# Attention and two mixture layers on one core: three rows of a step table are moved, the softmax sums are normalised at other steps, and a key difference on GpSimd is cut in two halves

## The chip, the cores and the metric

The kernel runs on one core of a Trainium2 chip, in one launch. The metric is device time in microseconds (us), from the start to the end of the execution; shorter is better. The engines are TensorE (PE in the profile, its weight loads PEld), VectorE (DVE), ScalarE (ACT), GpSimd (POOL) and SyncE (SP), which here only issues transfers: every DMA of the kernel goes through SP's queue, in program order.

## The reference

Three blocks, one after the other, in float32. The change is in the first.

```python
q_pool = q.reshape(B, H, S // 2, 2, D).mean(axis=3)          # B, H, S, D = 4, 8, 1152, 64
scores = 1/sqrt(D) * q_pool @ k.transpose(0, 1, 3, 2)
scores = scores - max(scores, axis=-1)
attn = exp(scores); attn = attn / (sum(attn, axis=-1) + 1e-09)
out = attn @ v                                               # 576 pooled queries, 1152 keys per head
...
x = out.transpose(0, 2, 1, 3).reshape(B, 576, 512)           # then two mixture layers of matmuls on x
```

## The kernel before

**Pairs and steps.** The 32 heads are worked in 16 pairs P = 0 to 15. A pair has 9 steps, one for each score tile of up to 128 queries by 1152 keys, so there are 144 steps; "step 3 of a pair" is step 9P + 3 (the diff calls them slots). One loop (line 568) writes each step out by hand, all engines in program order: in step s PE transposes the exponentials of tile s (L338), DVE and ACT copy the transposed thirds out of PSUM (L367), PE makes the scores of tile s + 2 (L304) into the PSUM banks that these copies have just freed, DVE takes their row maximum (L316, `smax`), ACT the exponentials (L328). In most steps PE also multiplies exponentials with values (L379, `pv`), 3 to 5 products of two heads each; some steps have none.

**Exact products in two parts.** Queries and keys are split in a high part, which the matmul takes as it is, and the rest. For a pair this is done one pair ahead, on POOL, in these steps: `qs` adds the two rows that are pooled (L232), `kh` cuts the keys (L197), `kl` is the difference keys minus cut keys (L200, tile kn, 128x1152), `qx` scales the queries (L239), `qh` cuts them (L197), `ql` is the difference of the queries (L200, tile qn). Then SP copies the parts to where the matmuls want them: `km`, four DMAs for the keys (L277, L278, tiles kt), and eight DMAs behind `ql` for the queries (L249 to L263, tiles q and qc). The keys and queries of the pair after that are loaded by `lqk` (L222, L223).

**Where a step's extra work stands.** The table `PREP` lists the steps at which these are issued: `(o, hook, name, ...)` means step o of the pair before; hook 0 is ahead of the step, hook 1 in its middle, hook 2 at its end. The first row of the table is for odd pairs (so it is worked during even ones), the second for even pairs. `CONV` is a like list for the conversion of the later layers' weights from float64, 20 pieces: a load by SP into tile cv (L122), an absolute value on ACT (L126), four bit operations on DVE (L129, L133, L137, L141), a rounding on ACT (L145), a difference on POOL (L149), and two stores by SP (L153, L154).

**Normalising.** When a pair's tiles are done, `norm1` takes the reciprocal of its 9 columns of sums on DVE: three small instructions (L393, L394, L395). SP then stores them in four DMAs to DRAM (L398) and reads them back spread over partitions in three (L407 to L409, tile rb). `norm2` multiplies the pair's output with that on POOL (L415). `NORM` says at which step `norm1` stands, counted from the pair's own first step, for even and odd pairs.

There is no scheduler: an engine does its instructions in the order in which this loop writes them, and waits only on semaphores.

Of the kernel before, what the change touches and what calls it, by code (L numbers as in the profile page):

```python
# [26 lines left out]
NP = NB * NH // 2  # L27
KT = S // 128
# [14 lines left out]
COPY = (('act', 'dve', 'act'), ('dve', 'act', 'act'), ('act', 'dve', 'dve'), ('dve', 'dve', 'act'))  # L43
SHORT = (0, 14, 16)
CLO = 'pool'
NORM = ((9, 2), (10, 2))

PREP = (
    ((-1, 2, 'qs', 'pool'), (1, 0, 'kh', 'pool', 0, 1), (1, 2, 'kl', 'pool', 0, 1), (2, 2, 'qx', 'pool'), (2, 2, 'qh', 'pool'), (2, 2, 'km', 0), (2, 2, 'km', 1), (3, 0, 'ql', 'pool'), (5, 0, 'lqk'), (15, 2, 'lv')),
    ((-1, 2, 'qs', 'pool'), (0, 2, 'kh', 'pool', 0, 1), (0, 2, 'kl', 'pool', 0, 1), (1, 2, 'qx', 'pool'), (2, 0, 'qh', 'pool'), (2, 0, 'km', 0), (2, 0, 'km', 1), (2, 2, 'ql', 'pool'), (5, 0, 'lqk'), (15, 2, 'lv')),  # L50
)

CONV = ((1, 2), (2, 1), (3, 2), (4, 1), (5, 2), (5, 2), (6, 1), (8, 1), (9, 2), (10, 1), (12, 1))
# [11 lines left out]
def attn_moe_kernel(ctx: ExitStack, tc: tile.TileContext, qT, kT, vP, muk, mur, wk, wv, wr, wth, wtr, wti, wch, ident, out):  # L65
    nc = tc.nc
    pe, act, dve, pool, sp = nc.tensor, nc.scalar, nc.vector, nc.gpsimd, nc.sync
# [90 lines left out]
    def attention(first):  # L158
# [258 lines left out]
        NT = NP * KT  # L417
# [3 lines left out]
        def at(slot, fn, *args):  # L421
            sched.setdefault(slot, []).append((fn, args))
# [13 lines left out]
        for P in range(NP):  # L436
            for g, (a, w, *when) in enumerate(groups):
                j = 0
                for o, m in when[P % 2]:
                    n = min(P * KT + o, NT)  # L440
                    plan.setdefault(n, []).extend(((P, g), j + x) for x in range(m))
                    j += m
                (at_mid if (n + 1) % 18 in SHORT else at_gap)(n + 1, pv_copy, (P, g))
            o, hook = NORM[P % 2]
            (at_gap, at_mid, at)[hook](min(P * KT + o, NT), norm1, P)
            at(n + (3 if P < NP - 1 else 6), norm2, P)
        last_slot = NT + 1

        def run_pv(s):
# [594 lines left out]
    with tc.manual_schedule():  # L1044
        dve.memset(hpi, math.pi / 2)
        act.activation(warm, hpi, AF.Exp)
        WR = [wr_tile(k).rearrange("p (a b) -> p a b", a=2) for k in range(4)]
        first = weight_pieces("wr", wr, 512, lambda name, k: WR[k], 512) + weight_pieces("wk", wk, 512, in_dram, 512)
        first += weight_pieces("wv", wv, 512, in_dram, 512)
        attention(first)  # L1050
# [37 lines left out]
```

## Time and profile before

| what | value |
|---|---|
| time before, median of 3 runs | 986.11 us (983.55 to 988.0) |
| the profiled execution's own time | 986.29 us |
| its span, first to last instruction | 984.2 us |
| PE busy | 958.6 us, 97% of the span |
| DVE, ACT, POOL busy | 694.9, 552.6, 450.7 us |
| the steps of attention | up to about 490 us of the span |

The profile is of one execution. A row that begins with an engine's name is a group or an instruction; `[1.15 <-DVE E L367]` behind a row of the timeline means that the engine stood idle for 1.15 us before it, and that the DVE instruction of line 367 which writes tile E ended the wait. `SPq` is an instruction of the queue of SP, that is, the issue of a DMA.

### The profile page before, as it was taken

To read this page: it belongs to the slowest core of one execution; us is meant where nothing else is said; L and a number is where in the kernel's file an instruction comes from. 1 tells how busy PE (TensorE), PEld (TensorE's weight loads), DVE (VectorE), ACT (ScalarE), POOL (GpSimd) and SP (SyncE) were. 2 spreads that over 40 slices of the span, in tenths; PEclk is the share of its full clock that TensorE was granted. 3 is DMA by queue.
4 is the path that set the end of the run, shared out by engine and by line. 5 is a ranking of instruction groups with operands and counts; after the bars stand their busy time and mean duration, and the time that the engine had idled before them with its cause. 6 is when DMAs were issued, how large, how long until landed. Compare 5 with 4: busy or idle time off the path is not lost.

```text
span 984.2 us, 18354 instructions
## 1 busy us (share of the span) xinstructions
PE 958.6 (97%) x6832; PEld 839.7 (85%) x6832; DVE 694.9 (71%) x1043; ACT 552.6 (56%) x1174; POOL 450.7 (46%) x454
## 2 busy tenths in 40 slices
PE   6999999999999999999999999999999999999998
PEld 4777777877777777777788999999999999999998
DVE  7577877787787788777747888878636755576622
ACT  5667666776666666667755566555535443343410
POOL 5314535234353234531226666555646666475731
PEclk8999999999999999999999999999999999999999
DMA  6666647866667775767373333323402501010001
GB/s 159 179 178 154 178 148 217 224 168 180 199 189 225 203 185 177 215 182 176 135 290 98 108 99 96 98 82 123 174 1 69 210 1 49 1 43 8 25 26 49
DMA packets 65641, 130.85 MB, mean 133 GB/s; under 512 B 14800, under 2 KB 33744, under 8 KB 65552
## 3 DMA queue, kind: packets, MB, share of 16 engines
q1 hardware_dynamic: 65552, 129.68, 45.4%
q8 instruction: 54, 0.88, 0.4%
q14 instruction: 35, 0.29, 0.1%
HBM read 70.98 MB, written 22.68 MB: 95 GB/s over the span
## 4 chain that ended last, share of the span: by engine, by line
PE 82%; DMA 6%; DVE 4%; SPq 4%; ACT 2%; POOL 1%; issue 1%; ACTq 0%; DVEq 0%; POOLq 0%
PE sc L304 13%; PE ps L981 12%; PE pv L379 11%; PE ps L731 10%; PE ps L750 10%; PE sc L338 8%; PE ps L1000 5%; PE ps L927 5%; PE ps L702 4%; PE tx L338 3%; DMA cv<-wv 2%; DVE m L316 1%; DMA q<-qn 1%; DMA cv<-wk 1%; DVE r L393 1%
## 5 line engine op out<-in xcount | busy, mean ns | idle before, releaser
L316 DVE TENSOR_REDUCE m<-sc 128x1 f32<-128x1152 f32 x144 | 195.4, 1357 | 71.7 <-PE sc L304 70.6
L328 ACT ACTIVATE e<-sc,m 128x1152 f32<-128x1152 f32 x144 | 176.0, 1222 | 76.4 <-DVE m L316 74.8
L304 PE MATMUL sc<-kt,q 128*128 128x384 f32 (+1 forms) x864 | 196.0, 354 | 14.6 <-DVE E L367 4.3
L304 PEld LDWEIGHTS sc<-kt,q 128*128 128x128 f32 (+1 forms) x864 | 143.5, 188 | 23.9 <-DVE E L367 6.2
L338 PEld LDWEIGHTS sc<-idn,e 128*128 128x128 f32 x864 | 98.3, 141 | 35.6 <-issue 27.7
L338 PE MATMUL sc<-idn,e 128*128 128x128 f32 x864 | 122.9, 279 | 2.3 <-ACT e L328 2.2
L981 PE MATMUL ps<-b,a 128*128 128x288 f32 x816 | 111.7, 296 | 0.0
L981 PEld LDWEIGHTS ps<-b,a 128*128 128x128 f32 x816 | 109.8, 188 | 0.6
L731 PE MATMUL ps<-x,a 128*128 128x288 f32 x768 | 105.7, 298 | 1.8 <-POOL x L682 1.5
L731 PEld LDWEIGHTS ps<-x,a 128*128 128x128 f32 x768 | 103.8, 191 | 2.6 <-POOL x L682 2.0
L750 PE MATMUL ps<-k,b 128*128 128x288 f32 x768 | 103.7, 295 | 0.0
L750 PEld LDWEIGHTS ps<-k,b 128*128 128x128 f32 x768 | 102.3, 188 | 0.3
L232 POOL TENSOR_TENSOR qn<-qn 128x576 f32<-128x576 f32 x15 | 22.1, 1476 | 145.4 <-DMA qn<-qT 85.5
L379 PE MATMUL pv<-M,vn 128*64 128x320 f32 x576 | 84.4, 438 | 0.0
L338 PE MATMUL tx<-idn,e 128*128 128x128 f32 x432 | 71.5, 275 | 0.5 <-DVE E L367 0.5
L379 PE MATMUL pv<-E,vn 128*64 128x256 f32 x576 | 71.0, 386 | 0.0
L379 PEld LDWEIGHTS pv<-M,vn 128*64 128x64 f32 x576 | 38.5, 136 | 36.1 <-issue 7.7
L718 POOL TENSOR_TENSOR k<-h,k 128x288 fp32r<-128x288 f32 x64 | 56.6, 900 | 19.5 <-ACT k L717 17.1
L367 ACT COPY M<-sc 128x384 f32<-128x384 f32 x104 | 46.0, 481 | 31.9 <-PE sc L338 31.9
L682 POOL TENSOR_TENSOR x<-t,x 128x288 fp32r<-128x288 f32 x56 | 47.9, 872 | 34.5 <-ACT x L681 32.6
L367 ACT COPY E<-sc 128x384 f32<-128x384 f32 x89 | 39.6, 481 | 42.0 <-PE sc L338 42.0
L149 POOL TENSOR_TENSOR cv<-cv 128x512 fp32r<-128x512 f32 x16 | 20.9, 1308 | 85.9 <-ACT cv L145 78.7
(128 smaller groups left out, 1649.4 us busy)
## 6 DMA issues: line engine op xcount, KB each, us to landing
vn<-vP SPq DMA_DIRECT2D x16, 576.0 KB
kt<-kh SPq DMA_DIRECT2D x31, 288.0 KB
kn<-kT SPq DMA_DIRECT2D x15, 576.0 KB
qn<-qT SPq DMA_DIRECT2D x15, 576.0 KB
kt<-kn SPq DMA_DIRECT2D x30, 288.0 KB
q<-qn SPq DMA_DIRECT2D x30, 288.0 KB
q<-qn SPq DMA_DIRECT2D x30, 256.0 KB
b<-wtk SPq DMA_DIRECT2D x9, 576.0 KB
```

Of the source, the lines that this page charges most:

```text
L304: r = pe.matmul(sc[0:m, c, 0:384], lhsT=x, rhs=k[:, 384 * c:384 * c + 384], start=(i == 0), stop=(i == len(ops) - 1),)
L316: r = dve.tensor_reduce(m, scs[n][:, :, 0:384], axis=AX.XY, op=ALU.max, negate=True)
L328: r = act.activation(e, sc[:, :, 0:384], AF.Exp, bias=m, scale=1.0, accum_out=rss[P][:, t:t + 1])
L338: r = pe.transpose(ps[:, 128 * j:128 * j + 128], es_[n][:, c, 128 * j:128 * j + 128], idn)
L367: r = (act.copy if e == "act" else dve.tensor_copy)(out, ps)
L379: pe.matmul(pvs[k][64 * h:64 * h + 64, :w], lhsT=vns[P][:, h, j], rhs=e, start=(x == 0), stop=(x == KT - 1))
L718: pool.tensor_tensor(q[:, 1], h, q[:, 0].bitcast(F32), ALU.subtract)
L731: pe.matmul(ps, lhsT=WK[k, f // 4][:, w, 128 * (f % 4):128 * (f % 4) + 128], rhs=x[k][:, c], start=(k == 0 and n == 0), stop=(k == 3 and n ...
L750: pe.matmul(pss[d], lhsT=WV[f][:, w, 128 * d:128 * d + 128], rhs=k2[f][:, c], start=(f == 0 and n == 0), stop=(f == 7 and n == 2))
L927: pe.matmul(ps, lhsT=y[k // 2][:, k % 2, x], rhs=WT[k][:, w], start=(k == 0 and p == 0), stop=(k == 3 and p == 2))
L981: pe.matmul(pss[d], lhsT=zs[j][z][:, 128 * d:128 * d + 128], rhs=WTK[min(j, 8)][:, w, cs], start=(m == 0 and n == 0), stop=(m == 8 and n = ...
L1000: pe.matmul(ps, lhsT=WC[k][:, w, 128 * d:128 * d + 128], rhs=us[c0, k][:, x], start=(k == 0 and n == 0), stop=(k == 3 and n == 2))
```

## The change

Numbers in three tables change, and how far ahead of `norm2` its `norm1` stands; no instruction's work does, but that `kl` is issued as two instructions of 576 columns.

```diff
-NORM = ((9, 2), (10, 2))
+NORM = ((13, 2), (16, 2))
...
-    ((-1, 2, 'qs', 'pool'), (1, 0, 'kh', 'pool', 0, 1), (1, 2, 'kl', 'pool', 0, 1), (2, 2, 'qx', 'pool'), (2, 2, 'qh', 'pool'), (2, 2, 'km', 0), (2, 2, 'km', 1), (3, 0, 'ql', 'pool'), (5, 0, 'lqk'), (15, 2, 'lv')),
...
+    ((-1, 2, 'qs', 'pool'), (1, 0, 'kh', 'pool', 0, 1), (1, 2, 'kl', 'pool', 0, 2), (1, 2, 'kl', 'pool', 1, 2), (2, 0, 'km', 0), (2, 0, 'km', 1), (2, 2, 'qx', 'pool'), (2, 2, 'qh', 'pool'), (2, 2, 'ql', 'pool'), (5, 0, 'lqk'), (15, 2, 'lv')),
...
-            at(n + (3 if P < NP - 1 else 6), norm2, P)
+            at(min(P * KT + o, NT) + (4 if P < NP - 1 else 6), norm2, P)
```

The second row of `PREP` changes in the same way. `norm1` of an even pair moves from step 0 to step 4 of the odd pair that follows, `norm1` of an odd pair from step 1 to step 7 of the even pair that follows; for the last pair nothing moves. `norm2` moves from step 5 of the pair that follows to its step 8 for an even pair, and from step 6 to step 2 of the pair after that for an odd one.

On DVE, the end of step 0 of pair 7, before (r is a tile of `norm1`, m the maxima, cv a weight piece, E the exponentials):

```order
L316 TENSOR_REDUCE m<-sc_121 128x1
L393 TENSOR_SCALAR r_140<-rs_137 128x9
L394 RECIPROCAL r_140<-r_140 128x9
L395 STREAM_TRANSPOSE rt<-r_140 128x32
L133 TENSOR_SCALAR cv<-cv 128x512
L367 COPY E<-sc_120 128x3x128
L137 SCALAR_TENSOR_TENSOR cv<-cv 128x512
```

The same place now:

```order
L316 TENSOR_REDUCE m<-sc_121 128x1
L133 TENSOR_SCALAR cv<-cv 128x512
L367 COPY E<-sc_120 128x3x128
L137 SCALAR_TENSOR_TENSOR cv<-cv 128x512
L316 TENSOR_REDUCE m<-sc_120 128x1
```

The end of step 4 now, from the copy ahead of it:

```order
L367 COPY M<-tx 128x3x2x64
L316 TENSOR_REDUCE m<-sc_121 128x1
L393 TENSOR_SCALAR r_140<-rs_137 128x9
L394 RECIPROCAL r_140<-r_140 128x9
L395 STREAM_TRANSPOSE rt<-r_140 128x32
L367 COPY M<-sc_120 128x3x128 x2
```

The bit operation L133 is now first behind the maximum, and `norm1` stands where two copies follow it and no bit operation.

On SP's queue, pair 14, before: the seven DMAs of `norm1` of pair 13 are ahead of the copies of keys and queries for pair 15.

```order
L398 DMA scr<-rt 9x32 x4
L407 DMA rb<-scr 64x576
L408 DMA rb<-scr 64x512
L409 DMA rb<-scr 64x64
L277 DMA kt<-kh 64x1152
L278 DMA kt<-kn 64x1152
L277 DMA kt<-kh 64x1152
L278 DMA kt<-kn 64x1152
L249 DMA q_1_0_125<-qn 64x1152
```

Now these copies come first; behind the last of them there follow a weight load, the values' load, two stores and only then `norm1`'s:

```order
L263 DMA qc_128<-qn 64x64 x2
L122 DMA cv<-wv 128x1024
L228 DMA vn<-vP 128x1152
L153 DMA wv_93<-cv 128x512
L154 DMA wv_93<-cv 128x512
L398 DMA scr<-rt 9x32 x4
L407 DMA rb<-scr 64x576
```

In an odd pair `norm1`'s seven DMAs moved likewise, and stand now between the last L263 and the loads L222 and L223.

On POOL the order of a pair's preparation stays. `ql` of odd pairs now comes ahead of the weight difference (L149) of its step, where there is one; for even pairs, `norm2` of an odd pair now stands between `qh` and `ql`.

## Rows read from the trace of the kernel before

**Rows 1.** The page's first part: busy time and share of the span.

```profile
span 984.2 us, 18354 instructions
PE 958.6 (97%) x6832; PEld 839.7 (85%) x6832; DVE 694.9 (71%) x1043; ACT 552.6 (56%) x1174; POOL 450.7 (46%) x454
```

**Rows 2.** Busy time by stretch; last columns granted clock, DMA share, GB/s.

```profile
34.00:490.00 456.00, 446.10 (x3215) 347.52 (x3213) 354.44 (x459) 311.84 (x575) 164.94 (x123) 1.00 0.67 184
```

**Rows 3.** Waits of PE from 34 to 490 us: total, times, longest.

```profile
PE sc L304 <- DVE E L367: 3.5, 3, 1.3
PE sc L304 <- DMA q<-qn: 3.0, 2, 1.8
PE sc L304 <- ACT M L367: 1.9, 1, 1.9
PE sc L304 <- ACT E L367: 1.1, 2, 0.7
```

**Rows 4.** Timeline of all engines, 226.2 to 231 us (pair 7, step 0).

```profile
226.27 2.64 POOL L200 TENSOR_TENSOR kn<-kn,kh 128x1152 f32<-128x1152 f32 x1
226.29 2.64 DVE L393 TENSOR_SCALAR r<-rs 128x9 f32<-128x9 f32 x1
229.22 0.21 DVE L395 STREAM_TRANSPOSE rt<-r 128x32 f32<-128x32 f32 x1
229.86 0.54 DVE L367 COPY E<-sc 128x384 f32<-128x384 f32 x1
230.45 0.64 PEld L304 LDWEIGHTS sc<-kt,q 128*128 128x128 f32 x4 [1.47 <-DVE E L367]
230.46 0.79 PE L304 MATMUL sc<-kt,q 128*128 128x384 f32 x3 [1.15 <-DVE E L367]
```

**Rows 5.** All instructions of line 393: shortest, median, longest in ns.

```profile
L393 DVE TENSOR_SCALAR r<-rs x16: 164/501/2644, 50.3 to 494.3; 128x9 f32<-128x9 f32 x16
```

**Rows 6.** Timeline of PE at 157 to 160 us: the first scores of pair 5.

```profile
159.21 0.97 PE L304 MATMUL sc<-kt,q 128*128 128x384 f32 x4 [1.26 <-DMA q<-qn]
```

**Rows 7.** Timelines of POOL, 438 to 445, and SP, 439 to 463 us (pair 14).

```profile
440.57 1.46 POOL L200 TENSOR_TENSOR qn<-qn 128x576 f32<-128x576 f32 x1
...
440.29 1.37 SPq L398 DMA_DIRECT2D scr<-rt  x4
448.16 1.33 SPq L249 DMA_DIRECT2D q<-qn  x1
456.01 0.59 SPq L122 DMA_DIRECT2D cv<-wv  x1
```

**Rows 8.** Timelines of ACT, 461 to 464, and PE, 461 to 465 us (pair 14, step 8).

```profile
461.70 0.66 ACT L126 ACTIVATE cv<-cv 128x512 f32<-128x512 f32 x1 [1.96 <-DMA cv<-wv]
...
463.98 0.62 PE L304 MATMUL sc<-kt,q 128*128 128x384 f32 x2 [1.86 <-ACT M L367]
```

**Rows 9.** Timelines of POOL, DVE, PE, 239 to 248 us (pair 7, steps 4 and 5).

```profile
241.92 1.28 POOL L149 TENSOR_TENSOR cv<-cv 128x512 fp32r<-128x512 f32 x1 [9.64 <-ACT cv L145]
...
240.61 1.36 DVE L316 TENSOR_REDUCE m<-sc 128x1 f32<-128x1152 f32 x1 [0.21 <-PE sc L304]
242.46 1.02 DVE L367 COPY M<-sc 128x384 f32<-128x384 f32 x2 [0.50 <-PE sc L338]
...
242.84 1.32 PE L304 MATMUL sc<-kt,q 128*128 128x384 f32 x6
```

**Rows 10.** Timelines of POOL, DVE, PE, 217 to 223 us (pair 6, steps 7 and 8).

```profile
219.96 1.28 POOL L149 TENSOR_TENSOR cv<-cv 128x512 fp32r<-128x512 f32 x1 [7.21 <-ACT cv L145]
...
218.76 1.36 DVE L316 TENSOR_REDUCE m<-sc 128x1 f32<-128x1152 f32 x1 [0.33 <-PE sc L304]
220.58 0.43 DVE L385 COPY xt<-pv 128x256 f32<-128x256 f32 x1 [0.46 <-PE pv L379]
221.05 0.56 DVE L367 COPY M<-sc 128x384 f32<-128x384 f32 x1
...
221.42 1.52 PE L304 MATMUL sc<-kt,q 128*128 128x384 f32 x6
```

More of the change, by code (lines that the diff above doesn't have):

```diff
@@ L45 @@
 CLO = 'pool'
-NORM = ((9, 2), (10, 2))
+NORM = ((13, 2), (16, 2))
 PREP = (
-    ((-1, 2, 'qs', 'pool'), (1, 0, 'kh', 'pool', 0, 1), (1, 2, 'kl', 'pool', 0, 1), (2, 2, 'qx', 'pool'), (2, 2, 'qh', 'pool'), (2, 2, 'km', 0), (2, 2, 'km', 1), (3, 0, 'ql', 'pool'), (5, 0, 'lqk'), (15, 2, 'lv')),
-    ((-1, 2, 'qs', 'pool'), (0, 2, 'kh', 'pool', 0, 1), (0, 2, 'kl', 'pool', 0, 1), (1, 2, 'qx', 'pool'), (2, 0, 'qh', 'pool'), (2, 0, 'km', 0), (2, 0, 'km', 1), (2, 2, 'ql', 'pool'), (5, 0, 'lqk'), (15, 2, 'lv')),
+    ((-1, 2, 'qs', 'pool'), (1, 0, 'kh', 'pool', 0, 1), (1, 2, 'kl', 'pool', 0, 2), (1, 2, 'kl', 'pool', 1, 2), (2, 0, 'km', 0), (2, 0, 'km', 1), (2, 2, 'qx', 'pool'), (2, 2, 'qh', 'pool'), (2, 2, 'ql', 'pool'), (5, 0, 'lqk'), (15, 2, 'lv')),
+    ((-1, 2, 'qs', 'pool'), (0, 2, 'kh', 'pool', 0, 1), (0, 2, 'kl', 'pool', 0, 2), (0, 2, 'kl', 'pool', 1, 2), (1, 2, 'km', 0), (1, 2, 'km', 1), (1, 2, 'qx', 'pool'), (2, 0, 'qh', 'pool'), (2, 2, 'ql', 'pool'), (5, 0, 'lqk'), (15, 2, 'lv')),
 )
```

## The prediction

> **What bounds the kernel now.** I began with the page's busy times: PE is busy for 958.6 of 984.2 us [rows 1], so only the 25.6 us in which it is idle can be won without taking work from it, and the change takes none. The change is all in attention, so I asked for the stretch from 34 us, behind the start, to 490 us, the end of the steps: 456.00 us, of which PE is busy 446.10, so idle 9.90 [rows 2]. That is the ceiling, 1.0% of the time. The waits of PE in this stretch tell what the 9.90 us are: 3.5 us in three waits for a copy by DVE, 3.0 in two for the copies of queries, 1.9 in one for a copy by ACT, 1.1 in two smaller ones for ACT [rows 3]; 0.4 us are spread over shorter gaps. PE's granted clock is 1.00 there [rows 2], its upper level, so the clock has no part in it. For each wait I went to the timeline, to see what the engine that PE waited for had done.
>
> **Waits for DVE (3.5 us).** At 226 us, step 0 of pair 7, DVE comes to `norm1`. Its first instruction, L393, works on 9 columns and took 2.64 us, from 226.29 to 228.93; on POOL `kl` (L200) runs from 226.27 to 228.91 [rows 4]. The shortest L393 took 0.164 us, the median 0.50 [rows 5]. So DVE stood for 2.5 us behind POOL's instruction, though no semaphore is between them. The copy of E, two instructions behind, came at 229.86, and PE, which needed that bank, stood for 1.15 us [rows 4]. The other two of the three waits are 60 and 120 us later, at the same step of pairs 9 and 11; that all three are 3.5 us is in [rows 3].
> The Trainium skill, SBUF — State Buffer, section Who interferes with whom, says that a DVE `tensor_scalar` with both ends in SBUF can use the port pair that it shares with GpSimd, and that the later of two then fully blocks until the first is done. By that rule L393 ends when L200 does, and the trace agrees to 0.02 us [rows 4]; the same rule speaks against the change too, since it blocks L393 behind any instruction of POOL, wherever it is moved.
> After the change, step 0 has no `norm1`. The bit operation that stands first in its place can be held by the same POOL work, but by no more than one half of `kl`, 2.64 / 2 = 1.3 us [rows 4], as POOL's instruction ends there. It is also spared `norm1`'s own time: from the end of L393 to the end of L395 there are 0.50 us [rows 4], with the shortest L393 0.66. So DVE comes out of the step at least 2.5 + 0.66 - 1.3 = 1.8 us earlier, more than the 1.15 us that PE lost. I take all 3.5 us as gone. (The weight loads stood a little longer, 1.47 us where PE shows 1.15 [rows 4], so the true loss may be 3.5 x 1.47 / 1.15 = 4.5 us.)
>
> **Waits for queries (3.0 us).** Pair 5's first scores waited 1.26 us for tile q [rows 6], pair 13's the rest of the 3.0 us [rows 3]. Pair 15's preparation, which goes the same way, shows why the copies are late: POOL is done with `ql` at 440.57 + 1.46 = 442.03, but SP issues `norm1`'s stores from 440.29, their read-backs and the keys' copies after that, and the first query copy at 448.16 [rows 7], 6.1 us after it could have gone. The change takes the seven DMAs out of the way, and puts the keys' copies ahead of `qx`, where they can go as soon as `kl` is done, while POOL works 2 us and more on the queries. So the query copies can start at `ql`'s end, some 6 us earlier in every odd pair. The waits are at most 1.8 us [rows 3]; they go. Even pairs, which show no such wait, gain the same. The loads of the pair after next are behind these copies, and in even pairs come earlier as well; in odd pairs `norm1`'s DMAs now stand ahead of them, which costs what they won. `norm2` between `qh` and `ql` waits for `norm1`'s read-back, which sets out four steps ahead of it; I cost it at nothing, since even pairs would have to lose their 6 us first.
>
> **Wait for ACT (1.9 us).** At 461.70 ACT's L126 had waited 1.96 us for a weight load, all that is behind it on ACT was late, and PE stood 1.86 us [rows 8]. That load was issued at 456.01, last in the queue behind pair 15's copies [rows 7]. With these some 6 us earlier, it lands before 461.70 - 1.96 = 459.7. Gone too. In all 3.5 + 3.0 + 1.9 = 8.4 us are taken away.
>
> **What the new places cost.** This is where I part from the plain sum. Steps 4 and 7 have no bit operation, but a short cover. In pair 7, step 4, the maximum ends at 241.97 and the next copies begin at 242.46; PE starts scores at 242.84, and needs the first copied bank two of six products later, 242.84 + 1.32 / 3 = 243.28. A free `norm1` of 0.66 us moves the first copy, half of 1.02 us, to 242.63 + 0.51 = 243.14: it just fits, so it costs nothing. But POOL's weight difference L149 stands there, from 241.92 to 243.20, and begins before L393 could [rows 9]. L393 would end at 243.20, `norm1` 0.50 later, the first copy at 244.21: PE waits 0.93 us. In pair 6, step 7, the maximum ends at 220.12 and L149 runs from 219.96 to 221.24; `norm1` would be done at 221.74, the copy L385 (0.43) and the copy of the bank (0.56) at 222.73, where PE needs it at 221.42 + 0.43 = 221.85 [rows 10]: 0.88 us. The conversion of weights has a period of eight pairs, so that pairs 14 and 15 repeat this, and the sum of the four is 2 x (0.93 + 0.88) = 3.6 us. At the eleven other places nothing of POOL's stood at that time in the trace of before. There POOL's preparation can come to stand, now that queries are loaded earlier in even pairs: between 0 and, at the four even pairs with a weight difference one step ahead, about half of such a wait, 4 x 0.45 = 1.8 us. I take 0 to 1.8 as the bound and 0.5 as the value, nearest to the many unharmed places. Cutting `kl` in two costs one more start on POOL per pair, for which the 64% of the stretch in which POOL is idle (164.94 of 456 busy [rows 2]) leave room: nothing. If that cover were gone, and a start cost as much as the shortest L393, 0.16 us [rows 5], 15 of them would be 2.4 us.
>
> **Sum.** 8.4 away, 3.6 + 0.5 new: 4.3 us won; with the higher reading of the waits for DVE 5.3. I take 5.0, for the high reading carries over to the other waits as well. The profiled execution took 986.29 us, so 981.3; it lies 0.2 us above the median 986.11, and so 981.1, in round numbers 981.
>
> **Rivals.**
> *The new places are free.* L149 and `norm1` could miss each other: at pair 7 they are 0.05 us apart (241.92 and 241.97 [rows 9]), and a DVE instruction that is first is not held. Then 8.4 to 9.9 us are won (all idle time of the stretch): 986.1 - 9 = 977. For it speaks the small distance at the odd pairs, against it that at pair 6 L149 is ahead by 0.16 us [rows 10].
> *New waits as dear as the old.* POOL's earlier work in even pairs meets `norm1` at step 7 in all seven of them and the four above keep theirs: 2 x 0.93 + 7 x 0.88 = 8.0 new against 8.4 gone. 985.5, no change that can be told.
> *Queries are late for another reason.* If it is the transfers and not their issue that are slow (the queues are busy 67% of the stretch [rows 2]), an earlier issue moves their landing less. Then the 3.0 us stay: 986.1 - 5.0 + 3.0 = 984.1. Against it: between 442.03 and 448.16 no query copy was under way at all [rows 7].
> *Slower.* In odd pairs SP now waits at `norm1`'s first store until DVE has done step 4, and the loads of keys and queries are queued behind it. If these loads then land late enough for the following preparation, done in even pairs, that the query copies lose more than the 6 us that they won, every odd pair's first scores wait longer. With copies 1.5 us later than before, that is 7 x 1.5 = 10.5 us more, less the 3.5 + 1.9 won elsewhere, and with the 4.1 at the new places: 986.1 + 9 = 995. It decides from the point at which SP is held at the store for over 6 us beyond the time at which it issued these loads before.
> The Trainium skill, DMA: Bandwidth & Descriptors, section Anatomy of one DMA, says that waits for semaphores are made by the issuing sequencer ahead of dispatch, so what is behind a waiting DMA in its queue waits too; by it the store does hold the loads. Rows 7 agree as far as they go: the eight DMAs behind the stores came after them, in order.
>
> **Chances.** My forecast 0.48, with its own range 978.5 to 983.5; the free places 0.20; new waits as dear 0.16; late queries 0.08; slower 0.08. A difference of 0.5%, 4.9 us, is about what a measurement of this kernel can tell from no change: faster is below 981.2, slower above 991.0. Half of the forecast's share and a little more lies below 981.2, with the free places some 0.47; slower 0.08; the rest, 0.45, within. For the range I go from the free places with all idle time won, 976, to the new waits as dear with a little on top, 986.5; less than 2 in 10 is left out, most of it the slower case.
>
> **What would show it.** In the changed kernel's trace: PE's waits from 34 to 490 us without a DVE wait at step 0 of pairs 7, 9 and 11, without a DMA wait on tile q at pairs 5 and 13, without ACT's wait at L126 in pair 14, step 8; the first query copy issued within 1 us of `ql`'s end in odd pairs; no L393 above 1.5 us, and L393 of about 1.2 us with a wait of PE behind it in pairs 6, 7, 14 and 15. I am wrong if PE's idle time in the stretch is under 3 or over 8 us, if a wait for q remains, or if PE's busy time itself changes.

## The result, and the profile after

The changed kernel takes 972.94 us, the median of four runs (971.16 to 977.12), against 985.64 us of four runs before: ratio 0.9874, 95% interval 0.9844 to 0.9903. So it is faster, by 12.7 us, where 5.0 were forecast. Its profiled execution took 971.99 us, 14.3 less than that of before. Ten single runs of the changed kernel, these four and six of the fifth experiment, lie between 971.2 and 978.8 us; the fifth experiment shows what differs between two of them. One more run of the kernel before, beside the first four experiments, took 1055.19 us at a mean granted clock of 0.848, and no comparison here uses it.

The page of the changed kernel begins with these lines (answering to [rows 1]):

```profile
span 969.9 us, 18358 instructions
PE 954.0 (98%) x6832; PEld 837.6 (86%) x6832; DVE 679.2 (70%) x1043; ACT 552.6 (57%) x1174; POOL 456.1 (47%) x469
```

The stretch from 34 to 490 us, as in [rows 2]; behind each engine's busy time stands its number of instructions:

```profile
34.00:490.00 456.00, 454.91 (x3294) 356.35 (x3293) 345.34 (x470) 318.40 (x594) 172.77 (x141) 1.00 0.69 193
```

PE is busy for 454.91 of the 456 us, and more of its instructions fit in, 3294 for 3215. Of the waits in [rows 3] only one of two for ACT is left (a wait of 0.3 us of a transpose, L338, is new):

```profile
PE sc L304 <- ACT E L367: 0.7, 1, 0.7
```

**Where the 14.3 us lie.** Row maxima (L316) mark the steps, one for each. The first row of each fence is, from the timeline of DVE, the maximum with which pair 1 begins; the second is the group of all 144, with the shortest, median and longest in ns and the start of the first and of the last. Before:

```profile
42.94 1.36 DVE L316 TENSOR_REDUCE m<-sc 128x1 f32<-128x1152 f32 x1 [0.21 <-PE sc L304]
...
L316 DVE TENSOR_REDUCE m<-sc x144: 1344/1358/1360, 8.7 to 487.5; 128x1 f32<-128x1152 f32 x144
```

After:

```profile
37.84 1.36 DVE L316 TENSOR_REDUCE m<-sc 128x1 f32<-128x1152 f32 x1 [0.21 <-PE sc L304]
...
L316 DVE TENSOR_REDUCE m<-sc x144: 1345/1358/1360, 8.9 to 471.1; 128x1 f32<-128x1152 f32 x144
```

The **start**, up to pair 1, went from 42.9 to 37.8 us; of the change only the preparation of pair 1 stands in it. The **steps** from there to the last maximum went from 444.6 to 433.3, that is 11.3 us less. The **tail** behind them went from 984.2 - 487.5 = 496.7 to 498.8, 2.1 more. 5.1 + 11.3 - 2.1 = 14.3.

**More than PE's idle time.** In the steps 11.3 us are won, where PE had 9.90 idle in the whole stretch [rows 2]. The row that explains it is that of the loads of weights (PEld) for the scores, from 43 to 488 us; behind the mean duration stands the idle time ahead of them. Before, and then after:

```profile
L304 PEld LDWEIGHTS sc<-kt,q 128*128 128x128 f32 (+1 forms) x804 | 131.9, 186 | 16.4 <-DVE E L367 4.8 <-DMA q<-qn 3.5 <-ACT M L367 2.5
```

```profile
L304 PEld LDWEIGHTS sc<-kt,q 128*128 128x128 f32 (+1 forms) x795 | 130.6, 186 | 5.0 <-DVE M L367 0.9 <-ACT M L367 0.3
```

The loads stood idle 11.4 us less. The three waits that I had priced at 3.5, 3.0 and 1.9 us of PE's idle time stand here with 4.8, 3.5 and 2.5. Counted gap by gap, those above 0.1 us between the two maxima, with those of the scores' other tiles (kh, qc), it is 13.6 before and 2.3 after, and the steps less this idle time are 431.0 us in both. For the ten profiles (the times come from three series of runs, the first two rows, experiments 1 to 4 and 5 to 8, and only within one were they taken side by side):

| kernel | time, median (runs) | start | steps | PE idle in the steps | L304 loads idle | steps less loads' idle |
|---|---|---|---|---|---|---|
| before | 985.64 (4) | 42.9 | 444.6 | 9.8 | 13.6 | 431.0 |
| after | 972.94 (4) | 37.8 | 433.3 | 0.7 | 2.3 | 431.0 |
| 1: both `norm1`, old `PREP` | 976.26 (4) | 43.3 | 436.5 | 2.5 | 5.9 | 430.6 |
| 2: new `PREP`, old `norm1` | 984.93 (10) | 43.6 | 441.2 | 7.2 | 10.3 | 430.9 |
| 3: `norm1` a little later | 981.61 (4) | 41.9 | 439.3 | 4.6 | 9.1 | 430.2 |
| 4: `kl` whole | 978.30 (4) | 42.7 | 434.5 | 1.6 | 3.7 | 430.8 |
| 5: as after | 977.72 (6) | 43.1 | 433.4 | 0.7 | 2.4 | 431.0 |
| 6: start's difference halved | 972.63 (6) | 38.6 | 433.9 | 1.2 | 3.0 | 430.9 |
| 7: even `norm1` alone | 988.17 (1) | 44.7 | 443.2 | 7.5 | 10.7 | 432.5 |
| 8: odd `norm1` alone | 976.22 (1) | 41.7 | 435.3 | 1.8 | 4.4 | 430.9 |

But for 7 (see there) the last column lies within 0.8 us, while the steps less PE's own idle time lie between 432.6 and 434.8. So the idle time of the loads is what the steps lose, and PE's own shows 72% of it before, 30% after, and from 29 to 70% elsewhere. Why PE's busy time covers the rest (the ends of its rows are modelled) was not tried. The Trainium skill, Perfetto Trace Analysis, section Identifying the Most-Contended Engine, says that the matmuls' busy share is not a good measure of how close a kernel is to its peak, since pipelined matmuls look smaller in the trace, and names the rate of matmul work and the busy share of the weight loads instead; the table agrees in that PE's busy time misleads, but what counts here is the idle time ahead of the loads.

**The new places.** Pair 7, step 4, where `norm1` now stands (to be held against [rows 9]):

```profile
232.12 1.36 DVE L316 TENSOR_REDUCE m<-sc 128x1 f32<-128x1152 f32 x1 [0.21 <-PE sc L304]
...
233.40 0.16 DVE L393 TENSOR_SCALAR r<-rs 128x9 f32<-128x9 f32 x1
233.44 1.28 POOL L149 TENSOR_TENSOR cv<-cv 128x512 fp32r<-128x512 f32 x1 [8.68 <-ACT cv L145]
```

Pair 6, step 7 (against [rows 10]):

```profile
211.80 1.36 DVE L316 TENSOR_REDUCE m<-sc 128x1 f32<-128x1152 f32 x1 [0.21 <-PE sc L304]
...
213.07 0.17 DVE L393 TENSOR_SCALAR r<-rs 128x9 f32<-128x9 f32 x1
213.11 1.27 POOL L149 TENSOR_TENSOR cv<-cv 128x512 fp32r<-128x512 f32 x1 [8.57 <-ACT cv L145]
```

The meeting that I foresaw takes place, but L393 comes 0.04 us ahead of L149, isn't held, and is over before it could matter. At pairs 14 and 15 it is the same (445.39 against 445.43, 466.63 against 466.67). It is no chance of one run: in the seven profiles in which L393 and L149 meet with nothing added (after, experiments 1 and 4 to 8) they meet 25 times, and each time L393 is 0.035 to 0.040 us ahead. All sixteen L393 (as [rows 5]):

```profile
L393 DVE TENSOR_SCALAR r<-rs x16: 161/164/589, 59.3 to 477.9; 128x9 f32<-128x9 f32 x16
```

**The queries' copies.** Timelines of POOL and SP, 425 to 436 us (pair 14, as [rows 7]):

```profile
429.28 1.42 POOL L200 TENSOR_TENSOR qn<-qn 128x576 f32<-128x576 f32 x1
...
428.54 0.77 SPq L278 DMA_DIRECT2D kt<-kn  x1
430.73 0.46 SPq L249 DMA_DIRECT2D q<-qn  x1
```

The keys' copies are issued when `ql` ends, at 429.28 + 1.42 = 430.70, and the first query copy goes 0.03 us later, where it had waited 6.1. Over the 14 later pairs it had gone 2.0 to 9.7 us after `ql`; now it goes 0.03 us after it in 12 of them, and 0.57 and 1.39 in two even ones.

### The profile page after: what moved, and what is told of

Same layout as the page of the kernel before. It is cut to its first block, busy times and chain, and to the rows that moved or that the text cites. A ratio compares the mean times of both kernels' runs of the same rounds, so it can differ in the third digit from the quotient of the medians.

```text
span 969.9 us, 18358 instructions
## 1 busy us (share of the span) xinstructions
PE 954.0 (98%) x6832; PEld 837.6 (86%) x6832; DVE 679.2 (70%) x1043; ACT 552.6 (57%) x1174; POOL 456.1 (47%) x469
## 4 chain that ended last, share of the span: by engine, by line
PE 94%; DVE 2%; DMA 1%; ACT 1%; issue 1%; SPq 0%; POOL 0%; ACTq 0%; POOLq 0%; DVEq 0%
PE sc L304 16%; PE pv L379 15%; PE ps L981 12%; PE ps L731 11%; PE ps L750 10%; PE sc L338 10%; PE ps L1000 5%; PE ps L927 5%; PE tx L338 5%; PE ps L702 4%; DVE m L316 1%; DMA a<-wth 1%; PE ps L885 1%; DMA kn<-kT 0%; ACT e L328 0%
## 5 line engine op out<-in xcount | busy, mean ns | idle before, releaser
L316 DVE TENSOR_REDUCE m<-sc 128x1 f32<-128x1152 f32 x144 | 195.4, 1357 | 67.4 <-PE sc L304 65.1
L304 PE MATMUL sc<-kt,q 128*128 128x384 f32 (+1 forms) x864 | 192.5, 351 | 4.2 <-DVE M L367 2.5
L304 PEld LDWEIGHTS sc<-kt,q 128*128 128x128 f32 (+1 forms) x864 | 142.0, 186 | 10.9 <-DVE M L367 3.7
L338 PEld LDWEIGHTS sc<-idn,e 128*128 128x128 f32 x864 | 97.2, 140 | 37.4 <-issue 28.5
L338 PE MATMUL sc<-idn,e 128*128 128x128 f32 x864 | 121.9, 277 | 3.7 <-ACT e L328 3.7
L338 PE MATMUL tx<-idn,e 128*128 128x128 f32 x432 | 70.7, 273 | 0.0
L379 PEld LDWEIGHTS pv<-M,vn 128*64 128x64 f32 x576 | 38.6, 136 | 36.1 <-issue 7.7
L415 POOL TENSOR_TENSOR xt<-xt,rb 128x576 f32<-128x576 f32 x16 | 22.9, 1432 | 98.8 <-DMA rb<-scr 56.7
L149 POOL TENSOR_TENSOR cv<-cv 128x512 fp32r<-128x512 f32 x16 | 21.2, 1327 | 96.3 <-ACT cv L145 96.3
```

The source lines that it names most:

```text
L304: r = pe.matmul(sc[0:m, c, 0:384], lhsT=x, rhs=k[:, 384 * c:384 * c + 384], start=(i == 0), stop=(i == len(ops) - 1),)
L316: r = dve.tensor_reduce(m, scs[n][:, :, 0:384], axis=AX.XY, op=ALU.max, negate=True)
L338: r = pe.transpose(ps[:, 128 * j:128 * j + 128], es_[n][:, c, 128 * j:128 * j + 128], idn)
L379: pe.matmul(pvs[k][64 * h:64 * h + 64, :w], lhsT=vns[P][:, h, j], rhs=e, start=(x == 0), stop=(x == KT - 1))
```

## The experiments

The first four ran side by side with 12 runs of the kernel before (983.7 to 988.8), the last four with 11 (median 986.73). Fences that give waits are of the stretch from 34 to 490 us. "Steps" and "start" are the table's.

**1. Both `norm1` moved, preparation as before.** The table `NORM` and the place of `norm2` as in the change, the table `PREP` as before.

```diff
-    (... (1, 2, 'kl', 'pool', 0, 2), (1, 2, 'kl', 'pool', 1, 2), (2, 0, 'km', 0), ...
+    (... (1, 2, 'kl', 'pool', 0, 1), (2, 2, 'qx', 'pool'), (2, 2, 'qh', 'pool'), (2, 2, 'km', 0), ...
```

> Only the normalising of sums is moved (steps 4 and 7); the preparation of keys and queries is as before, its key difference in one piece, its copies behind it. Theory A (the moved DMAs and the moved L393 make the whole gain): PE's waits for DVE at step 0 of pairs 7, 9 and 11, for q at pairs 5 and 13, and for ACT in pair 14 are all gone, PE idle from 34 to 490 us falls from 9.9 to under 2 us, time 9 to 12 us below before. Rival B (the preparation's new order and the halves are needed too): the bit operation that stands in norm1's place is held by the whole key difference, up to 2.6 us, and PE still waits some 1 us at step 0 of odd pairs; idle 3 to 5 us, time 5 to 8 us below before.

976.26 us, ratio 0.9899 (0.9865 to 0.9933); steps 436.5, 8.1 less than before. PE is idle for 2.9 us from 34 to 490 us, more than the 2 of theory A and just under the 3 of rival B. The one group over 0.3 us of its waits of PE that is new:

```profile
PE sc L304 <- DVE M L367: 1.7, 3, 0.7
```

The waits for queries and for ACT's weights, and those for DVE at step 0, are gone without the new `PREP`, and the query copies go at `ql`'s end as in the changed kernel; the three new waits for DVE are at step 7 of pairs 2, 8 and 10. At pair 8 the timeline of POOL and DVE has

```profile
276.36 2.64 POOL L200 TENSOR_TENSOR kn<-kn,kh 128x1152 f32<-128x1152 f32 x1
...
277.71 1.31 DVE L393 TENSOR_SCALAR r<-rs 128x9 f32<-128x9 f32 x1
```

`norm1` in its new place is held by the whole `kl` until that ends, at 279.00; at pairs 2 and 10 it is held likewise behind `kh` (L197) and `qs` (L232). So moving `norm1` is most of the gain, and the other part of the change removes some waits that this one brings.

**2. New preparation, `norm1` where it was.** The other half alone.

```diff
-NORM = ((13, 2), (16, 2))
+NORM = ((9, 2), (10, 2))
...
-            at(min(P * KT + o, NT) + (4 if P < NP - 1 else 6), norm2, P)
+            at(n + (3 if P < NP - 1 else 6), norm2, P)
```

> Only the preparation changes: key difference in two halves, key copies ahead of the queries' splitting; norm1 stays at steps 0 and 1, so its seven DMAs still stand ahead of the copies. Theory A: no L393 above 1.4 us, so the 3.5 us of waits for DVE go or fall below 1 us; the waits for q (3.0) and for ACT (1.9) stay, since the queue is as late as before. Time 3 to 4 us below before. Rival B (the early key copies are what makes the queries early): waits for q go as well, time 7 us or more below before.

984.93 us, ratio 0.998 (0.9966 to 0.9995); steps 441.2, 3.4 less than before. Waits of PE from 34 to 490 us, and the group of L393:

```profile
PE sc L304 <- DMA q<-qn: 4.1, 2, 2.7
PE sc L304 <- ACT M L367: 1.5, 1, 1.5
...
PE sc L304 <- DVE E L367: 0.4, 2, 0.2
...
L393 DVE TENSOR_SCALAR r<-rs x16: 161/486/1386, 51.0 to 491.6; 128x9 f32<-128x9 f32 x16
```

The waits for queries stay (4.1 for 3.0), and the first query copy of a pair still goes 0.8 to 9.5 us behind `ql` (pair 1's apart), so `km` ahead of `qx` doesn't free the queue: moving `norm1`'s DMAs does. The waits for DVE fall from 3.5 to 0.4, since L393 is held by one half of `kl` (1386 ns) and no longer by all of it (2644 [rows 5]). At pair 7, step 0, one comes during the first half:

```profile
226.60 1.41 POOL L200 TENSOR_TENSOR kn<-kn,kh 128x576 f32<-128x576 f32 x1
...
227.27 0.77 DVE L393 TENSOR_SCALAR r<-rs 128x9 f32<-128x9 f32 x1
...
227.97 1.41 POOL L200 TENSOR_TENSOR kn<-kn,kh 128x576 f32<-128x576 f32 x1
```

It ends at 228.04, with the first half (228.01), and doesn't wait for the second. Apart, the two parts take 8.1 and 3.4 us from the steps, together 11.3. That this nearly adds up is in part luck: each part alone removes the waits for DVE at step 0, and what is so counted twice is made up by the new waits of experiment 1, which the whole change doesn't have.

**3. `norm1` a little later.** Two one-column memsets on DVE ahead of L393, so that L149 is first where the two meet.

```diff
+            for _ in range(2):
+                dve.memset(r2[:, 31:32], 0.0)
```

> The changed kernel with two very short DVE instructions (a column of the sums' tile set to zero again) ahead of each norm1, so that L393 comes some 0.15 us later. Theory A (whoever comes first holds the other): in pairs 6, 7, 14 and 15 the weight difference on POOL is now first, L393 takes about 1.2 us there instead of 0.16, and PE waits 0.8 to 0.9 us behind each: 3.6 us in all, time 2 to 5 us above the changed kernel. Rival C (the new places have more cover than I reckoned): L393 is just as long, but PE waits under 0.2 us each, time within 1 us of the changed kernel. Rival D (no lock; L393 was long for another reason): L393 stays at 0.16 us.

981.61 us, ratio 0.9953 (0.9935 to 0.9971); steps 439.3, 6.1 more than after. Its lines stand 2 further down, so that L395 is `norm1`'s first instruction. Waits of PE, and the timeline at pair 7, step 4:

```profile
PE sc L304 <- DVE M L367: 3.6, 5, 0.8
...
238.67 1.28 POOL L149 TENSOR_TENSOR cv<-cv 128x512 fp32r<-128x512 f32 x1 [9.57 <-ACT cv L145]
...
238.78 1.19 DVE L395 TENSOR_SCALAR r<-rs 128x9 f32<-128x9 f32 x1
...
240.97 0.30 PEld L304 LDWEIGHTS sc<-kt,q 128*128 128x128 f32 x2 [1.10 <-DVE M L367]
240.97 1.08 PE L304 MATMUL sc<-kt,q 128*128 128x384 f32 x4 [0.78 <-DVE M L367]
```

The two memsets are 0.12 us of DVE's time at each `norm1` (59 ns each), and cost 6.1 us in all. L395 begins 0.11 us behind L149 and ends when that does, at 239.95 to 239.97, 1.03 us later than it would have; PE waits 0.78 us, the loads 1.10. This is the story that I had predicted for the change itself, with its price: 0.68 to 0.78 us of PE at each of the four places named, for the predicted 0.88 and 0.93. The fifth wait, 0.79 us at step 7 of pair 8, was not foreseen: there L395 begins at 278.39, behind the second half of `kl` (from 278.26), and takes 1.30 us; in the changed kernel it came ahead of that half and took 0.19. So the 3.6 us in all, as expected, are five smaller waits for four: in part luck. The Trainium skill, SBUF — State Buffer, section Who interferes with whom, has it that the engine which issues first keeps the shared pair for the whole instruction, and the other blocks; the trace agrees in both orders, with 0.16 us for L393 when it is 0.04 ahead, and 1.19 when it is 0.11 behind.

**4. `kl` in one piece.** All of the change but the halves.

```diff
-(1, 2, 'kl', 'pool', 0, 2), (1, 2, 'kl', 'pool', 1, 2)
+(1, 2, 'kl', 'pool', 0, 1)
```

> The changed kernel with the key difference in one piece again. Theory A: the bit operation at step 0 of odd pairs is held up to 2.6 us in place of 1.3, which the cover of 2.9 us of products there takes; PE idle from 34 to 490 us under 1 us, time within 2 us of the changed kernel. Rival B: PE waits 0.5 to 1 us at step 0 or 8 of most pairs, time 3 to 8 us above the changed kernel.

978.30 us, ratio 0.9918 (0.9901 to 0.9934); steps 434.5, 1.2 more than after, in one new wait of PE for DVE, 0.9 us, at pair 8, step 7. No wait at step 0 comes back, as theory A has it; PE is idle for 1.9 us from 34 to 490, not under 1. POOL and DVE there:

```profile
275.02 2.65 POOL L200 TENSOR_TENSOR kn<-kn,kh 128x1152 f32<-128x1152 f32 x1
...
276.17 1.52 DVE L393 TENSOR_SCALAR r<-rs 128x9 f32<-128x9 f32 x1
```

Halving is worth 1.2 us here once `norm1` stands at its new places (0.6 against the 433.9 of experiment 6, whose steps are the changed kernel's). The other 4.9 us by which this profile differs (a start of 42.7 for 37.8) could be the whole `kl` of pair 1, which is worked in the start, or not the kernel's at all; that led to the next two.

**5. The changed kernel again.** Two import lines are exchanged, no instruction differs:

```diff
+import math
 from contextlib import ExitStack
 
-import math
```
The question was whether the start of 37.8 us belongs to the change.

> The changed kernel once more, as it is (two import lines exchanged). Theory F (the changed kernel's profiled start, 5 us shorter than before's, is a matter of which of POOL and DVE comes first, and not of the change): the start, to the first row maximum of pair 1, falls on either 37 to 38 us or 42 to 44 us in this profile, and the single times lie in two groups some 5 us apart, about 972 and 977. Rival G (the change shortens the start): 37 to 38 us here too, and all times near 972. From pair 1's first row maximum to the last one: 433 us, as in its first profile, by either.

977.72 us (975.30 to 978.79, six runs), ratio 0.9918 (0.9891 to 0.9946). The steps repeat to 0.1 us (433.4), the start doesn't: 43.1, as before. Rival G is refuted. Two groups of times, as theory F has it, don't stand out: the ten runs of this kernel go from 971.2 to 978.8 with no gap over 2 us. What differs, in the timelines of POOL, DVE and PE at 9 to 17 us, is a race of the same kind. In this run:

```profile
9.71 1.40 POOL L492 TENSOR_TENSOR qn<-qn 64x576 f32<-64x576 f32 x1 [0.24 <-DMA qn<-qT]
11.07 2.87 POOL L200 TENSOR_TENSOR kt<-kn,kh 64x1152 fp32r<-64x1152 f32 x1
...
10.27 4.02 DVE L500 SCALAR_TENSOR_TENSOR q<-qn,q 64x320 fp32r<-64x320 f32 x2
...
14.34 0.62 PE L304 MATMUL sc<-kt,q 128*128 128x384 f32 x2 [1.32 <-DVE q L500]
```

and in the changed kernel's first profile:

```profile
9.09 1.16 POOL L197 TENSOR_SCALAR kh<-kn 64x1152 fp32r<-64x1152 f32 x1 [6.09 <-DMA kn<-kT]
10.22 1.74 POOL L492 TENSOR_TENSOR qn<-qn 64x576 f32<-64x576 f32 x1
11.92 2.90 POOL L200 TENSOR_TENSOR kt<-kn,kh 64x1152 fp32r<-64x1152 f32 x1
...
10.22 2.08 DVE L500 SCALAR_TENSOR_TENSOR q<-qn,q 64x320 fp32r<-64x320 f32 x2
...
10.71 1.60 DVE L500 SCALAR_TENSOR_TENSOR q<-qn,q 64x320 fp32r<-64x320 f32 x1
...
12.72 0.60 PE L304 MATMUL sc<-kt,q 128*128 128x384 f32 x2
```

The row with x2 holds two L500; the 10.71 row is the second of them by itself. In this run POOL's L492 is ahead of the first, which ends at 11.46, and its difference of the first keys (L200) begins at 11.07, ahead of the second (11.47), which is held until that ends; the pair takes 4.02 us. In the first profile the keys' load landed later (POOL waited 6.09 us for it; 5.32 in this run), and L492 began together with the first L500, which took 0.47. The second, from 10.71, took 1.60: it ends 0.34 us behind L492 (11.96), so it was held by that alone, and L200 came behind it, at 11.92. So something is held in both profiles, and the pair takes 2.08 or 4.02 us; in all ten the second L500 ends 0.34 to 0.36 us behind the POOL instruction that began ahead of it. PE then waits 1.32 us or not at all. The windows from 15 to 20 us have, in this run and then in the first profile of the changed kernel,

```profile
15.00:20.00 5.00, 3.81 (x16) 3.71 (x17) 3.80 (x5) 3.49 (x7) 1.73 (x2) 0.66 0.46 182
```

```profile
15.00:20.00 5.00, 3.90 (x28) 3.17 (x26) 4.66 (x6) 2.91 (x8) 1.09 (x4) 1.00 0.56 220
```

a granted clock of 0.66, so partly at the lower level of 1.2 GHz, against 1.00; 16 matmuls stand in the one and 28 in the other. In the profile of before POOL's difference also began at 11.07 and the two L500 took 4.28. In all ten profiles the two go together: where the two L500 took 3.6 to 4.3 us (eight profiles) the start is 41.7 to 44.7, where they took 2.08 and 2.48 it is 37.8 and 38.6. So one kernel has both starts, and the 5.1 us are no part of what the change does in the steps, though they are in the 14.3 between the two profiles. Whether the change makes the short start more frequent, no run tells; of the kernel before, one run of the eleven beside this experiment took 978.97 us, 4.2 less than the next.

**6. The start's difference halved too.** As L200 at the start was suspected, it is cut in two halves in the changed kernel, like `kl`.

```diff
-            cut_lo("pool", kt1[h1], k[h1], kh[h1])
+            for c in (left, right):
+                cut_lo("pool", kt1[h1, c], k[h1, c], kh[h1, c])
```

> The changed kernel, and at the start the key difference of the second head (line 200, tile kt, 2.9 us on POOL) in two halves. Theory F: the second query rest on DVE (line 500) waits for one half of it at most, PE's first scores of tile 2 begin some 1.4 us earlier where POOL comes first, the granted clock does not fall at 13 us, and the start is 38 to 40 us in every run: times near 972 and less spread, 3 to 5 us below the changed kernel where that had the long start. Rival H (the start is bound by the loads and by the other waits, 1.8 us for the first exponentials and 2.3 us at step 1): time within 1 us of the changed kernel.

972.63 us, ratio to the kernel before 0.9876 (0.9845 to 0.9907), 5.1 us below the changed kernel's six runs beside it; five of its six runs are at 974 or less, of the ten runs of the changed kernel three. Start 38.6.

```profile
12.29 1.67 POOL L200 TENSOR_TENSOR kt<-kn,kh 64x576 fp32r<-64x576 f32 x1
...
10.19 2.48 DVE L500 SCALAR_TENSOR_TENSOR q<-qn,q 64x320 fp32r<-64x320 f32 x2
```

The two L500 take 2.48 us, and PE doesn't wait for them. In this profile POOL came late as well (12.29), so the trace doesn't show a half holding the second L500, and the order of the first profile, with the whole L200, would have done the same. PE's granted clock fell all the same, for 3.4 us from 11.9, where theory F had it not fall. That halves bound the loss in the other five runs is not shown; the times, 0.5% below those of the changed kernel beside it, speak for it.

**7 and 8. Each `norm1` alone.** In the kernel before, with its `PREP`: only that of even pairs moved, and only that of odd pairs, each with its `norm2`.

```diff
-NORM = ((9, 2), (10, 2))
+NORM = ((13, 2), (10, 2))
```

> The kernel before, with norm1 and norm2 of even pairs alone moved (to steps 4 and 8 of the odd pair). Theory A: the DVE waits at step 0 of pairs 7, 9 and 11 go (3.5 us shown), the waits for q at pairs 5 and 13 (3.0) and for ACT in pair 14 (1.9) stay, since in even pairs the seven DMAs are still ahead of the copies; PE idle from 34 to 490 us 5 to 7 us. Rival B: the loads in odd pairs, now behind the DMAs, make the waits for q longer than 4 us.

988.17 us, one run, within the runs of the kernel before beside it (978.97 to 988.58); steps 443.2, only 1.4 less than before.

```profile
PE sc L304 <- DMA q<-qn: 4.2, 2, 2.6
PE sc L304 <- DVE E L367: 2.2, 3, 1.8
PE sc L304 <- ACT M L367: 1.1, 1, 1.1
...
440.39 2.63 POOL L200 TENSOR_TENSOR kn<-kn,kh 128x1152 f32<-128x1152 f32 x1
...
440.75 2.55 DVE L133 TENSOR_SCALAR cv<-cv 128x512 uint32<-128x512 uint32 x1
```

The waits at step 0 of pairs 7, 9 and 11 are gone, but at pair 14 a bit operation takes 2.55 us beside the whole `kl`, and PE waits 1.80 for the copy behind it. The waits for queries stay, and their 4.2 us meet rival B's mark of 4. The wait for ACT is no longer in pair 14 but in pair 6, and PE is idle for 8.2 us from 34 to 490, above the 5 to 7 expected. Behind the wait of 1.80 PE's granted clock is 0.50, its lower level, for 3.4 us from 445.3; no other profile has that in its steps. With it go the 1.5 us by which this row of the table stands above the others, so the gain in the steps would be nearer 3 us by an estimate from the table (1.4 + 1.5).

```diff
-NORM = ((9, 2), (10, 2))
+NORM = ((9, 2), (16, 2))
```

> The kernel before, with norm1 and norm2 of odd pairs alone moved (to step 7, and step 2 of the pair after). Theory A: the waits for q and for ACT in pair 14 go, the DVE waits at step 0 of odd pairs stay at 3 to 4 us shown; PE idle from 34 to 490 us 4 to 6 us.

976.22 us, one run; steps 435.3, 9.3 less than before.

```profile
PE sc L304 <- DMA q<-qn: 0.4, 1, 0.4
...
PE sc L304 <- DVE E L367: 0.2, 1, 0.2
```

The queries' and ACT's waits go, as expected, but for 0.4 us at one place; PE is idle for 2.2 us, where 4 to 6 were expected. That the waits for DVE at step 0 of odd pairs would stay was wrong: `norm1` still stands there, but isn't held for long. The timelines of pair 7 show why:

```profile
221.87 2.65 POOL L200 TENSOR_TENSOR kn<-kn,kh 128x1152 f32<-128x1152 f32 x1
...
223.92 0.63 DVE L393 TENSOR_SCALAR r<-rs 128x9 f32<-128x9 f32 x1
```

`kl` is 4.4 us earlier than in [rows 4] and L393 only 2.4: with the queue free in even pairs, the loads issued there (L222, at 209.09 for 216.70 before) seem to land earlier, and POOL begins its preparation sooner: ahead of `qs` (L232) it stands idle for 2.40 us before, and not at all here. So the odd `norm1` makes most of the gain, and the even one, moved on top of it, costs 1.2 us as long as `kl` is whole (steps 435.3 here, 436.5 in experiment 1, whose three waits stand at step 7; one profile of each). How it brings these about was not followed.

## Why the prediction was right or wrong

**What was right.** The direction and the mechanisms. L393's 2.64 us were a stand behind POOL and no work (experiments 1 to 3), though no semaphore is between the two; that an engine waits only on semaphores, as is said of the kernel before, does not hold for DVE beside POOL. The waits for queries came from `norm1`'s DMAs ahead of the copies in SP's queue (experiments 1 and 8 against 2 and 7), and the copies now go at `ql`'s end. ACT's wait at L126 fell with them. The loads that stand behind `norm1`'s store, the rival *Slower*, made PE wait nowhere, nor did any other wait at the queue. Each of the rows named as signs was found, but for the last, an L393 of 1.2 us in pairs 6, 7, 14 and 15.

**The step that failed: what the new places cost.** 3.6 + 0.5 = 4.1 us were charged, 0 were paid in the two profiles of the changed kernel; the rival "the new places are free" had this right. I put the earliest begin of `norm1` in pair 7 at 241.97, the end of the maximum's row, and L149 0.05 us ahead of it. But on DVE the next instruction begins 0.08 us before that row's end: after the change L393 begins at 233.40, where the maximum's row ends at 232.12 + 1.36 = 233.48. The trace of before has the same, 0.076 to 0.086 us, all 101 times that an instruction follows a maximum at once. By that, DVE was free at 241.89, 0.03 ahead of L149. In pair 6 the same 0.08 would not have been enough against 0.16; there L149 came 1.31 us behind the maximum's begin where it had been 1.20 ([rows 10] and the fence above), which fits that the maximum waited 0.21 us for PE in place of 0.33. Experiment 3 shows that all else in this step held: let L149 be first, and the four waits stand where they were foreseen and cost about what was said. So the order was wrong and not the price, and it was no toss: the 25 meetings went the same way. The 0.5 for the other places was not idle either: in experiment 6, whose steps are the changed kernel's, L393 at step 7 of pair 12 comes 0.24 us behind `qs` (L232), takes 1.20 us, and PE waits 0.47. With the trace of before alone, an order within 0.05 us should have been given as open, with 981 and 977 as its ends, and not as one case. Two figures of the working are also off by little: in pair 6 a third of the 1.52 us shown is 0.51 and not 0.43, which makes that wait 0.80, and the rival *New waits as dear as the old* comes to 985.7 and not 985.5.

**A term mis-sized: the waits removed.** I priced them with PE's idle time, 8.4 us, where the loads show 4.8 + 3.5 + 2.5 = 10.8, and called the 9.90 of [rows 2] a ceiling. The loads of weights lost 13.6, and the steps gained 11.3, so that the range, whose lower end of 976 stood on that ceiling, was too high. The remark in the step on DVE, that 1.47 stands where PE shows 1.15, was the right reading, for all waits and not for one. It follows that "wrong if PE's busy time itself changes" was a bad test, since part of the wait is counted there as busy.

**What lay outside it.** With both corrected, 986.3 - 11.3 is 975.0. The rest, 5.1 us of start less 2.1 of tail, is not what was predicted, and the start differs between two profiles of one kernel (experiment 5). Beside the runs of experiment 5 the change is worth 9.0 us (0.9918). The tail took 497 to 499 us in all ten profiles; in the changed kernel's first profile PE's granted clock was at its lower level for 6.8 us from 504.9, before for 3.4 us at 521.5. That is not all of it, as the six other tails with 3.4 us go from 497.1 to 498.7; what makes them differ was not tried, and it stays open.

## What to carry to other kernels

Read a wait of PE from the idle time of its weight loads, and check it against the length of the stage: here that came out at 11.3 us, where PE's own idle time said 9. An instruction of a few columns on DVE costs what is left of the POOL instruction beside it, if it comes second; so place it where it comes first with a margin, or cut the POOL instruction in pieces. A lead of 0.04 us held here in all 25 meetings, but 0.12 us more ahead of it turned it, so ask what else is about to change on either engine. Before a gain is put down to a change, compare the stages that it doesn't touch, and profile the same kernel twice.

## What was not expected of the hardware

- A DVE instruction of 161 ns takes 1.19 us when it begins 0.11 us behind POOL's (experiment 3), and 0.16 when it begins 0.04 us ahead. 0.12 us of DVE work added ahead of each `norm1` made the steps 6.1 us longer.
- Between two halves of a POOL instruction, one right behind the other, a waiting DVE instruction gets in: in experiment 2 L393 came during the first half, at 227.27, and ended 0.03 us behind it, while the row of the second had begun. L393 took 1386 ns at most with halves, 2644 without.
- A `scalar_tensor_tensor` of DVE with both inputs in SBUF is held in the same way: two L500 took 4.02 and 4.28 us where each had a POOL instruction ahead of it (L492, L200), and 2.08 where only the second had one (L492).
- With one such hold at the start PE waited 1.32 us, its granted clock over the window from 15 to 20 us was 0.66 instead of 1.00, and the start became 5 us longer. How much of this is the clock's was not separated: the lower level stood for 6.8 to 10.2 us of the start in the eight profiles with a long one, for 3.4 us in the sixth experiment's, whose start is 38.6, and not at all in the first profile of the changed kernel.
